# Two channels to a matmul: kernel values, a wider 0/1 spread and a new start in a single-core attention and long-convolution kernel

## The chip, the cores and the metric

One core of one Trainium2 chip. The metric is the time of the kernel on the device in microseconds (us), median over its executions. A program on one core is repeated on the same chip beside the kernel before. Wherever a ratio stands, it is the mean time of one kernel's fast runs over the mean of the other's fast runs of the same rounds, so it is not quite the ratio of the medians quoted beside it; brackets give its 95% interval. A run over 1.5% above the fastest of its kernel counts as slow; the medians and ranges quoted hold slow runs too, the ratios do not. The granted clock is the TensorE clock that a run was given, as a share of full speed.

## The reference

Two independent parts share the core and their outputs are joined:

```python
def _A_ref(x, wqkv, wo):            # x: 1 x 2048 x 640, 32 heads of 20
    W, dil = 8, 2                   # each position sees 8 keys, 2 apart
    ...
    logits = jnp.einsum("bhsd,bhswd->bhsw", q, kg) * scale
    attn = _softmax(masked logits)
    o = jnp.einsum("bhsw,bhswd->bhsd", attn, vg)
    return o... @ wo

def _B_ref(u, A_re, A_im, B_re, B_im, C_re, C_im, log_dt, Dskip):   # u: 1 x 2048 x 640, N = 192 states
    dt = jnp.exp(log_dt)[:, None]
    logdA = dt * (A_re + 1j * A_im)
    dB = dt * (B_re + 1j * B_im)
    P = jnp.exp(logdA[:, :, None] * l[None, None, :])
    K = jnp.einsum("dn,dnl,dn->dl", Cc, P, dB).real      # the "kernel values": 640 x 2048
    y = irfft(rfft(u padded) * rfft(K padded))[:L]       # convolution by FFT
    return y + u * Dskip
```

The change is about K. The kernel writes the exponent l as a coarse plus a fine part, builds an X table (20 coarse entries) and a Y table (33 fine ones) for each channel on VectorE and ScalarE, and gets K as small matrix products X^T Y over the 192 states. 128 of the states fill the partitions, the other 64 of two channels share them.

## The kernel before

The parts that the argument touches. Steps are queued with `st(...)` and put out in the order of a long list, `ORDER` (cut here), that also sets the order on each engine.

```python
    psk = Lazy(lambda: psp.tile([128, 512], f32, name="ps_k"))     # one PSUM bank for all kernel values
    st(lambda: V.memset(psk()[:], 0.0))
    ...
        def go(hf):                                      # a "flip": transposes of 5 chunks on TensorE
            for c in range(NCH):
                ...
                if hf == 0:
                    MM(o, lhsT=nt[:, 0:128], rhs=rhs[:, 0:96], start=True, stop=True, ...)
                    continue
                MM(o[:, 0], lhsT=nt[:, 0:128], rhs=rhs[:, 96:128], start=True, stop=True, ...)
                for h in range(2):                       # two 64-row tiles
                    hs = slice(64 * h, 64 * h + 64)
                    MM(o[hs, 1:3], lhsT=nt[hs, 128:192], rhs=rhs[hs, hs], ..., tile_position=(64 * h, 64 * h))
    ...
    cst = tl("prep", [128, 2, 2, CW], bf16, "cs", tag="cs", bufs=4)   # generators; stored to DRAM
    ...
    def kgen(c):
        t0 = 0
        for nt in (11, 11, 10):
            ps = lambda nt=nt: psk()[:, 0:nt * NB].rearrange("p (t b) -> p t b", b=NB)

            def go(part, t0=t0, nt=nt, ps=ps):
                for i in range(nt):
                    for g in range(4):
                        hb = 64 * (g // 2)
                        rows, col, tp = (slice(0, 128), 32 * g, 0) if part < 2 else (slice(hb, hb + 64), 128 + 32 * (g % 2), hb)
                        MM(ps()[32 * g:32 * g + 20, i, :], lhsT=X[c]()[rows, part % 2, :, col + t0 + i],
                           rhs=Y[c]()[rows, :, part % 2, col + t0 + i], start=(part == 0 and i == 0), stop=(part == 3), tile_position=(tp, 32 * g), ...)

            for part in range(4):
                st(lambda part=part, go=go: go(part))
            st(lambda t0=t0, nt=nt, ps=ps: ACTE.copy(out=Kd[c]()[:, :, t0:t0 + nt], in_=ps().rearrange("p t b -> p b t")))
            t0 += nt
    ...
        for tq in range(4):                              # 0/1 spread: the K values put in place for the FFT
            ts = slice(8 * tq, 8 * tq + 8)
            ps = bank([128, 8, 8, 8], "ps_s", "b")

            def go(ts=ts, ps=ps):
                for j in range(8):
                    for n_, (w, par) in enumerate(plan[j]):
                        sel = slice(0, 8) if par is None else slice(par, 8, 2)
                        for g in range(4):
                            MM(ps()[32 * g:32 * g + 32, j, sel], lhsT=SEL()[:, w, :], rhs=K2()[:, g, sel, ts], ..., tile_position=(0, 32 * g))
    ...
        rc = tl("att", [128, 128], f32, "rc", tag="rc")          # reciprocals of the softmax
        hl = tl("att", [128, 2, 128], bf16, "rhl", tag="rhl")
```

Mind the last index of X and Y in `kgen`: a matmul takes one column (one state-channel slot) out of each of 20 and 33 rows of 192 elements. All its weight columns and all its moving columns are far apart in memory.

The softmax here doesn't subtract the row's maximum and nothing guards it: scores larger than these inputs give would overflow.

## Time and profile before

| | before |
|---|---|
| median of 4 (range) | 380.8 us (376.8 to 384.4) |
| span of the profiled run, granted clock | 376.6 us, 0.879 |
| busy TensorE / VectorE / ScalarE | 300.9 / 312.0 / 274.1 us |
| TensorE idle for instructions ("issue") before ps_k and ps_s | 9.2 and 8.8 us |

VectorE and TensorE are near equally loaded, and neither is full throughout. One stretch that the prediction reads but does not show, as busy time by stretches (from:to us and length; then TensorE, its weight loads, VectorE, ScalarE, GpSimd, each with its count; then granted clock, DMA share, GB/s):

```profile
23.00:60.00 37.00, 18.20 (x49) 6.23 (x49) 36.75 (x87) 34.20 (x88) 5.41 (x8) 0.69 0.69 194
```

VectorE is full (36.75 of 37) while TensorE is half idle.

### The profile page before, as it was taken

To read this page: it belongs to the slowest core of one execution; us is meant where nothing else is said; L and a number is where in the kernel's file an instruction comes from. 1 tells how busy PE (TensorE), PEld (TensorE's weight loads), DVE (VectorE), ACT (ScalarE), POOL (GpSimd) and SP (SyncE) were. 2 spreads that over 40 slices of the span, in tenths; PEclk is the share of its full clock that TensorE was granted. 3 is DMA by queue.
4 is the path that set the end of the run, shared out by engine and by line. 5 is a ranking of instruction groups with operands and counts; after the bars stand their busy time and mean duration, and the time that the engine had idled before them with its cause. 6 is when DMAs were issued, how large, how long until landed. Compare 5 with 4: busy or idle time off the path is not lost. (4 is left out here: it accounts for less than half of the span.)

```text
span 376.6 us, 14749 instructions
## 1 busy us (share of the span) xinstructions
PE 300.9 (80%) x6407; PEld 199.4 (53%) x6420; DVE 312.0 (83%) x468; ACT 274.1 (73%) x602; POOL 62.8 (17%) x123
## 2 busy tenths in 40 slices
PE   3982619989999794857596998889779997999791
PEld 2640204564346441645464786758557685657660
DVE  3379999979999899967866999994582998999970
ACT  2589997999996672456846877869575998977541
POOL 1101121100000000715032200120130102300641
PEclk9987588999999898558967897589899999999996
DMA  7996487763857556497725253325662998997947
GB/s 189 228 272 133 137 265 259 242 213 127 262 176 244 195 164 201 107 257 207 167 76 175 66 196 119 106 58 174 193 170 81 334 316 246 308 300 217 254 104 165
DMA packets 59696, 72.54 MB, mean 193 GB/s; under 512 B 24344, under 2 KB 49544, under 8 KB 58864
## 3 DMA queue, kind: packets, MB, share of 16 engines
q1 hardware_dynamic: 53760, 54.91, 49.0%
q0 software_dynamic: 5296, 15.96, 15.6%
q8 instruction: 50, 0.82, 0.9%
q10 hardware_dynamic: 576, 0.74, 0.6%
q14 instruction: 14, 0.11, 0.1%
HBM read 43.98 MB, written 24.98 MB: 183 GB/s over the span
## 5 line engine op out<-in xcount | busy, mean ns | idle before, releaser
L575 PE MATMUL ps_p<-xT,w 128*128 128x512 bf16 x287 | 75.6, 411 | 22.2 <-ACT st L578 19.7
L575 PEld LDWEIGHTS <-w 128*128 128x128 bf16 x300 | 30.0, 104 | 63.5 <-issue 34.3
L549 PE MATMUL ps_k<-Ytab,Xtab 128*20 128x33 bf16 (+1 forms) x2560 | 53.9, 246 | 11.4 <-issue 9.2
L736 DVE TENSOR_TENSOR prod<-qb,kb 128x2048 bf16<-128x2048 bf16 x40 | 47.7, 1222 | 16.9 <-PE ps_l L741 16.9
L549 PEld LDWEIGHTS <-Xtab 128*20 128x20 bf16 (+1 forms) x2560 | 45.4, 127 | 22.3 <-issue 18.5
L792 DVE TENSOR_TENSOR p<-vb,attn 128x2048 bf16<-128x2048 bf16 x40 | 47.6, 1221 | 11.3 <-PE ps_o L797 11.3
L634 ACT CAST A<-ps_f 128x512 bf16<-128x512 f32 x80 | 43.6, 611 | 18.0 <-PE ps_f L629 16.5
L688 ACT CAST S<-ps_f 128x512 bf16<-128x512 f32 x80 | 43.2, 618 | 10.1 <-PE ps_f L684 7.5
L578 ACT CAST st<-ps_p 128x512 bf16<-128x512 f32 x60 | 33.5, 583 | 6.3 <-PE ps_p L575 6.0
L785 POOL DMA_DIRECT2D vb<-vd x40 | 22.0, 555 | 80.3 <-DVE p L792 78.1
L691 DVE TENSOR_TENSOR Yf<-S 128x1024 bf16<-128x1024 bf16 x40 | 26.1, 686 | 6.5 <-PE ps_ia L705 5.0
L684 PE MATMUL ps_f<-A,cT 128*64 128x128 bf16 x640 | 27.7, 225 | 2.5 <-issue 1.6
L811 PE MATMUL ps_op<-wo,oT 128*128 128x320 bf16 x160 | 26.4, 308 | 0.0
L684 PEld LDWEIGHTS <-cT 128*64 128x64 bf16 x640 | 20.3, 111 | 11.2 <-issue 8.9
L510 ACT ACTIVATE Stab<-ta 128x192 bf16<-128x192 f32 x80 | 25.1, 366 | 0.6 <-DVE Ytab L532 0.6
L711 ACT CAST Z<-ps_ia 128x512 bf16<-128x512 f32 x40 | 22.0, 625 | 2.2 <-PE ps_ia L705 2.0
L741 PE MATMUL ps_l<-prod,cGs 128*32 128x512 bf16 x160 | 18.0, 445 | 7.0 <-DVE prod L736 5.9
L629 PE MATMUL ps_f<-cBD,U 128*64 128x128 bf16 x320 | 22.5, 302 | 0.0
L629 PEld LDWEIGHTS <-U 128*64 128x64 bf16 x320 | 19.6, 205 | 3.6 <-issue 2.8
L705 PE MATMUL ps_ia<-cEA,Yf 64*128 64x128 bf16 x640 | 21.2, 216 | 0.4 <-ACT Z L711 0.2
L188 DVE TENSOR_TENSOR krtmp<-Xtab,Xg 128x1536 bf16<-128x1536 bf16 (+2 forms) x30 | 20.6, 688 | 0.2
L188 DVE TENSOR_TENSOR Xtab<-Xtab,Xg 128x1536 bf16<-128x1536 bf16 (+2 forms) x30 | 20.5, 686 | 0.0
(105 smaller groups left out, 524.2 us busy)
## 6 DMA issues: line engine op xcount, KB each, us to landing
vb<-vd SPq DMA_DIRECT2D x40, 128.5 KB
vb<-vd POOLq DMA_DIRECT2D x40, 128.5 KB, 4.1
Gdram<-cs SPq DMA_DIRECT2D x22, 192.0 KB
HB<-k_HB SPq DMA_DIRECT2D x8, 512.0 KB
Zdram<-Z SPq DMA_DIRECT2D x3, 1024.0 KB
zq<-Zdram SPq DMA_DIRECT2D x12, 256.0 KB
kb<-kd SPq DMA_DIRECT2D x4, 657.5 KB
us<-in_B_u_dram POOLq DMA_DIRECT2D x2, 1280.0 KB, 7.4
```

Of the source, the lines that this page charges most:

```text
L188: step(lambda i=i: V.tensor_tensor(out=(O, t)[i]()[0], in0=Y(), in1=g(i), op=A.mult))
L549: MM(ps()[32 * g:32 * g + 20, i, :], lhsT=X[c]()[rows, part % 2, :, col + t0 + i], rhs=Y[c]()[rows, :, part % 2, col + t0 + i], start=(par ...
L575: MM(ps()[:], lhsT=w()[:, kt, 128 * ct:128 * ct + 128], rhs=xT()[:, kt, 512 * sc:512 * sc + 512], start=(kt == 0), stop=(kt == 4))
L578: st(lambda so=so, sc=sc, ps=ps: ACTE.copy(out=so()[:, sc], in_=ps()[:]))
L629: MM(ps()[64 * r:64 * r + 64, jj], lhsT=src(16 * dd + 4 * jq + jj), rhs=BD1()[:, r, :], start=(jj == 0), stop=True, skip_group_check=True, ...
L634: st(lambda o=o, ps=ps: ACTE.copy(out=A1[c]()[:, :, sig, o:o + 16].rearrange("p k (j g) -> p k j g", g=4), in_=ps()[:].rearrange("p j (k g ...
L684: MM(ps()[64 * dd:64 * dd + 64, kk, r], lhsT=T()[:, k, r, :], rhs=A1[c]()[:, k, :, 64 * dd:64 * dd + 64], start=(kk == 0 and r == 0), stop ...
L688: st(lambda h=h, ps=ps, Sp=Sp: ACTE.copy(out=Sp()[:, :, :, :, 2 * h:2 * h + 2, :].rearrange("p r s j k g -> p (r s) j k g"), in_=ps()[:].r ...
L691: st(lambda b=b, i=i, Sp=Sp: V.tensor_tensor(out=Yf[c]()[:, 2 * i:2 * i + 2, :, 32 * b:32 * b + 32], in0=Sp()[:, :, 1].rearrange("p r j k ...
L736: st(lambda pr=pr, ct=ct, u2=u2: V.tensor_tensor(out=pr()[:], in0=q()[:, ct].unsqueeze(1).to_broadcast([128, 4, PB]), in1=windows(k()[:, c ...
L792: st(lambda p2=p2, u2=u2: V.tensor_tensor(out=p2()[:], in0=v()[:, :, 2 * u2:2 * u2 + PB], in1=attn[b]()[:, u2].unsqueeze(1).to_broadcast([ ...
L811: MM(ps()[:], lhsT=oT[b]()[:, t, 128 * x:128 * x + 128], rhs=wo_sb()[:, t, 320 * eh:320 * eh + 320], start=(t == 0), stop=(t == 4))
```

## The change

Intent: fewer and wider TensorE instructions for K (two channels to a matmul, 40 by 66 columns, two column groups in place of four; a spread with 256 columns), so that TensorE neither issues nor fetches so many (12842 become 9224, by the prediction); a quicker start (matmuls clear the bank, flips grouped by tile shape); and an order made for the new durations. The larger Kd tile takes memory; in return one of four `cs` buffers goes, and the reciprocals share the output tiles' buffers.

```diff
-    st(lambda: V.memset(psk()[:], 0.0))
+    st(lambda: PQ.memset(zf()[:, 0:512], 0.0))
+    def clear():
+        for k in range(11):
+            MM(psk()[:], lhsT=zf()[:, 0:128], rhs=zf()[:, 0:512], start=True, stop=True)
 ...
-                    continue
-                MM(o[:, 0], lhsT=nt[:, 0:128], rhs=rhs[:, 96:128], ...)
+                else:
+                    MM(o[:, 0], lhsT=nt[:, 0:128], rhs=rhs[:, 96:128], ...)
+            for c in range(NCH if hf else 0):        # the 64-row tiles in a loop of their own
 ...
-    Kd = [tl("cst", [128, NB, 32], bf16, "Kd", tag="Kd") ...]
+    Kd = [tl("cst", [128, 2, 2, NB, 16], bf16, "Kd", tag="Kd") ...]
 ...
-            cst = tl("prep", [128, 2, 2, CW], bf16, "cs", tag="cs", bufs=4)
+            cst = tl("prep", [128, 2, 2, CW], bf16, "cs", tag="cs", bufs=3)
 ...
+        def pairs(ap, col):      # 40 weight columns, 96 elements apart: two channels
+            return bass.AP(ap.tensor, ap.offset + col, [list(ap.ap[0]), [96, 40]])
+        def two(ap, col):        # 33 x 2 moving columns, the pair 96 elements apart
+            return bass.AP(ap.tensor, ap.offset + col, [list(ap.ap[0]), list(ap.ap[1]), [96, 2]])
+        for gl in range(2):
+            for nt in (6, 5, 5):
+                        for q in range(2):
+                            rows, col, tp = (slice(0, 128), 32 * q + 16 * gl, 0) if part < 2 else (slice(64 * q, 64 * q + 64), 64 + 16 * gl, 64 * q)
+                            MM(ps()[64 * q:64 * q + 40, i], lhsT=pairs(X[c]()[rows, part % 2], col + t0 + i),
+                               rhs=two(Y[c]()[rows, :, part % 2], col + t0 + i), ..., tile_position=(tp, 64 * q))
 ...
-        for tq in range(4):
-            ps = bank([128, 8, 8, 8], "ps_s", "b")
+        for jp in range(4):
+            ps = bank([128, 2, 8, 2, 16], "ps_s", "b")
 ...
-        rc = tl("att", [128, 128], f32, "rc", tag="rc")
+        rc = tl("att", [128, 128], f32, "rc", tag="ob", bufs=2)
 ...  (hl the same; layouts of Gt, K2 and the DRAM copy of K to suit; ORDER wholly new)
```

The four products of a pair of channels include two mixed ones, which are not wanted and are simply not read.

## The prediction

A "change of mode" in it is a change of the tile shape from one matmul to the next, as between the 128-row and the 64-row ones of its timeline of the flips.

> **What bounds the kernel now.** I read the page's slices, then busy time by stretches, the chain of waits, the waits by engine, the timeline of TensorE, and the groups of instructions.
>
> By stretches (PE, PEld, DVE, ACT, POOL busy us, granted clock, DMA share, GB/s):
>
> ```profile
> 0.00:23.00 23.00, 16.38 (x122) 11.05 (x124) 8.94 (x20) 10.40 (x26) 3.39 (x11) 0.99 0.94 237
> ...
> 60.00:111.00 51.00, 47.40 (x675) 24.91 (x680) 47.83 (x88) 49.88 (x104) 3.89 (x6) 1.00 0.63 206
> 111.00:165.00 54.00, 44.03 (x1028) 27.58 (x1030) 52.15 (x78) 30.31 (x72) 7.64 (x20) 0.82 0.63 190
> 165.00:213.00 48.00, 35.37 (x948) 24.65 (x946) 34.85 (x42) 30.92 (x64) 14.99 (x28) 0.78 0.60 159
> ```
>
> Until 23 us VectorE has 8.9 us of work: it waits for the transposes ("flips") on TensorE. From 23 to 165 us VectorE is full (36.8 of 37, 47.8 of 51, 52.2 of 54). From 165 us no engine is full by its busy time: 35.4 and 34.9 of 48. The chain of waits says what holds it: from 213 us on it is nearly all TensorE, with holes that nothing in the program explains (start, length, what):
>
> ```profile
> 227.12 0.89 PE ps_k L549 x41
> 228.01 0.59 PE ps_f L629 x8
> 228.78 1.67 issue
> 230.45 0.94 PE ps_k L549 x33
> ...
> 240.74 1.83 PE ps_s L665 x73
> 242.57 1.21 PE ps_f L629 x10
> 243.78 2.25 issue
> ```
>
> The waits by engine put 8.8 us before ps_s L665 and 9.2 us before ps_k L549 down to "issue". In the trace's queue records each hole follows a packet of the instruction queue (50 packets, 0.82 MB, so 16 KB each): packets start at 228.05, 243.62, 265.88, 280.25 and 311.32 us, and TensorE goes on 1.3 to 1.6 us after each has landed. The holes are 256 TensorE instructions or a multiple apart. From 111 us on I count fourteen that I read so, some 26 us together, of which 25 come after 165 us or just before. So the second half is bound by TensorE, and a seventh of its time there is spent waiting for its own instructions. The holes come where instructions are short: 256 of them are 128 pairs of weight load and matmul, which ps_k uses up in 2.2 us and ps_s in 1.3, against about 4 us from one block to the next.
>
> [...] in the groups
>
> ```profile
> L684 PEld LDWEIGHTS <-cT 128*64 128x64 bf16 x640 | 20.3, 111 | 11.2 <-issue 8.9
> L629 PEld LDWEIGHTS <-U 128*64 128x64 bf16 x320 | 19.6, 205 | 3.6 <-issue 2.8
> L684 PE MATMUL ps_f<-A,cT 128*64 128x128 bf16 x640 | 27.7, 225 | 2.5 <-issue 1.6
> L549 PE MATMUL ps_k<-Ytab,Xtab 128*20 128x33 bf16 (+1 forms) x2560 | 53.9, 246 | 11.4 <-issue 9.2
> L665 PE MATMUL ps_s<-K,cSEL 128*32 128x64 bf16 (+1 forms) x720 | 9.9, 208 | 8.8 <-issue 8.8
> ```
>
> (the last numbers: busy us, mean ns of one, idle before) 64 weight columns take 111 ns when they are neighbours (T) and 205 when they are 64 bytes apart (U); and a ps_k matmul of 33 columns[...], takes longer (246) than one of 128 neighbours (225).[...]
>
> ```profile
> 8.83 0.24 PE L375 MATMUL ps_tr<-dg,nat 128*128 128x32 bf16 x1
> 9.00 0.32 PE L378 MATMUL ps_tr<-dg,nat 64*64 64x64 bf16 x2
> 9.24 0.24 PE L375 MATMUL ps_tr<-dg,nat 128*128 128x32 bf16 x1
> ```
>
> One chunk's three small matmuls take 0.41 us, with two changes of mode among them.
>
> **The change, part by part.**
>
> *Kernel values (ps_k).* 2560 matmuls of 20 by 33 columns in four column groups become 1280 of 40 by 66 in two. In the timeline, 40 full-height ones take 0.80 us (235.27 to the next group at 236.07) and 80 half-height ones 1.40 (238.17 to 239.57): 20 and 17.5 ns each with the change of mode, 16 to 17 within a burst, so 2560 x 18 = 46 us. A round of four thus takes 66 ns, and it is no slower at half the granted clock (means within a burst 16.8 and 17.0 ns). 33 columns in 66 ns are 2.0 ns a column, near U's weights (two loads a round, 62 ns a matmul, 64 columns in 124 ns: 1.9). I read this as a rate per stream of scattered columns: a matmul is bound by its 33 scattered reads. The new matmul reads 66 columns, scattered too (pairs 192 bytes apart), and only two run side by side: 66 x 1.66 (the rate of the shortest loads: 184 ns for U, 107 to 111 for ps_k, less the common 78) + 12 of turnaround = 122 ns a round, 61 a matmul, 1280 x 61 = 78 us. So halving the instructions makes this stage's matmuls **32 us longer**, not shorter. Half of them (1316 of 2560 by windows) lie in the TensorE-bound stretch: +16 us on the path. The others lie between 60 and 165 us, where TensorE has 14 us idle in 105: +15 fits barely, with VectorE still the bound.
>
> *Instruction blocks.* 12842 TensorE instructions become 9224, 50 blocks become 36, and the densest ones slow down: 128 pairs of the new ps_k take 7.8 us, longer than a block's 4 us. Holes in ps_k and ps_s should go; those amid other short matmuls (31 ns a pair, 4.0 us a block) stay at 0.3 us or so. 25 us become about 5: **-20 us** on the path.
>
> *0/1 spread (ps_s).* 720 matmuls at 8 to 12 ns, some 7 us, become 180 of 256 columns[...]. **-2 us**, its holes being counted above.
>
> *Flips.* 30 chunks of 0.41 us (0.31[...]) lie between 7.9 and 22.2 us. Grouped by shape, each half flip has one change of mode, not nine or ten[...] (the first flip waits until 6.4 us anyway). I estimate 1.0 us a half flip for 2.1 to 1.6, so 5 to 6 us for six; the flip that the phases need comes first. VectorE is full right after, so **-5 us** for all that follows.
>
> *ScalarE.* ps_k is emptied 30 times for 15. From 363 columns in 459 ns and 512 in 611, a column costs 1 ns: 10 x 490 + 20 x 425 = 13.4 us for 6.9. +6.5 us on an engine with 274 of 377: beside other work.
>
> *Transfers.* K2's pieces shrink from 512 to 256 bytes and Kd's store becomes four; hidden, DMA being at 0.6 there. The reciprocals share the output tiles' buffers: a wait of up to 3 us for an output to land, four times, partly on VectorE's path near the end. *New order*: unknown; it is made for the new durations, so I give it 2 us.
>
> Sum on the path: +16 - 20 - 2 - 5 - 2 + 2 (shared buffers) = -11 at best, less what VectorE and the wait for one ps_k bank keep back, which I put at 4: 376.6 becomes 369 or 370. Scaled by the median of 380.8 to that span of 376.6: 373 to 374. I go to 372 for the first rival.
>
> **The rivals.** (1) *The stage is bound by weight columns or by a fixed cost of a round, not by scattered moving columns.* Weight columns: 4 x 20 = 80 in 66 ns before, 2 x 40 = 80 after, so 42 us both times. For it: 0.83 ns a column is also near U's 0.97 if two loads share one path. Against: the shortest ps_k load is 107 ns where four shared ones would give 144. Then the +16 is nil, and VectorE (312 us and its start) is the bound: 354 to 362. (2) *TensorE becomes the bound in the first half too.* With +32 us it needs 301 + 32 - 8 = 325 of busy time plus early idle (some 18), holes (5) and an end where it has 11 idle: 360 at the least; if the ps_k bank is waited for 30 times, if the rate is 2.0 and not 1.66 (+8 us), or if the clock stays low, 380 to 390. For it: VectorE and TensorE are near equal already. (3) *The holes stay*, because a block takes its 4 us whatever the rate and other short matmuls fill in: then +16 - 8 - 7 gives 378. Against: holes stand at 1.3 to 1.6 us after landing, so slower use of a block must shorten them.
>
> **Range and chances.** The terms are large and of opposite sign (+16, -20), each known to some 6 us, so 80% is 356 to 386. 2% below is 373.2, so my estimate lies on that line; rival 1 falls wholly below it, at a quarter. Faster 0.55, same 0.34, slower 0.11.
>
> **What would show it.** Right: ps_k matmuls of some 280 to 300 ns for 246, spaced by about 60; "issue" before ps_s and ps_k below 4 us together; flips over by 16 us; ScalarE's ps_k group at 13 us for 30; VectorE's busy time unchanged at 312. Wrong: ps_k spaced by 33 ns (rival 1), holes of 2 us (rival 3), VectorE no longer full between 60 and 165 us (rival 2).

## More of the kernel before

The kernel before took 377 to 382 us in the different batches, so batches are compared by their ratios.

VectorE hardly waits up to 165 us, as the waits of VectorE between 23 and 165 us say (who waits, for whom: us in total, times, longest):

```profile
DVE cs L454 <- ACT cs L453: 2.6, 2, 2.3
DVE prod L736 <- PE ps_l L741: 1.7, 2, 1.0
DVE pr L414 <- PE ps_tr L378: 0.8, 1, 0.8
```

## The result, and the profile after

| | before | after |
|---|---|---|
| median (range), 4 runs each | 380.8 us (376.8 to 384.4) | 395.3 us (394.6 to 397.7) |
| ratio | | 1.0428 [1.0333, 1.0522] |
| span, granted clock of the profiled run | 376.6, 0.879 | 393.0, 0.901 |
| busy TensorE / VectorE / ScalarE | 300.9 / 312.0 / 274.1 | 336.8 / 313.1 / 280.5 |

The changed kernel is slower, by 4%, outside the predicted range. All its runs are fast ones and its granted clock is higher than before, so the clock is not the reason.

The instructions first. By the trace's records of the ps_k line (name and count: least/median/longest ns, first and last start), before and then after:

```profile
L549 PEld LDWEIGHTS <-Xtab x2560: 107/124/176, 68.6 to 290.6; 64*20 64x20 bf16 x99, 128*20 128x20 bf16 x98
L549 PE MATMUL ps_k<-Ytab,Xtab x2560: 222/244/270, 68.6 to 290.7; 64*20 64x33 bf16 x99, 128*20 128x33 bf16 x98
```

```profile
L572 PEld LDWEIGHTS <-Xtab x1280: 141/149/184, 68.7 to 301.3; 64*40 64x40 bf16 x93, 128*40 128x40 bf16 x90
L572 PE MATMUL ps_k<-Ytab,Xtab x1280: 276/291/351, 68.7 to 301.4; 64*40 64x66 bf16 x93, 128*40 128x66 bf16 x90
```

A matmul takes 291 ns for 244. What counts is how closely they follow each other within a burst, since several run side by side: the starts in the trace are 63.8 ns apart for full-height ones and 59.0 ns for half-height ones, where it was 17.1 and 15.9. (Counting the first and last matmuls of a burst in another way moves these spacings, and those below, by up to 3 ns.) So half as many cost almost four times as much each. One half-height burst of each, and the group after it, in the timeline of TensorE (start, length, count), before and then after: 80 matmuls hold TensorE for 1.40 us, then 12 for 0.84 us.

```profile
238.17 1.47 PE L549 MATMUL ps_k<-Ytab,Xtab 64*20 64x33 bf16 x80
239.57 0.72 PE L629 MATMUL ps_f<-cBD,U 128*64 128x128 bf16 x8
```

```profile
230.86 0.90 PE L572 MATMUL ps_k<-Ytab,Xtab 64*40 64x66 bf16 x12
231.70 0.40 PE L768 MATMUL ps_l<-prod,cGs 128*32 128x512 bf16 x4
```

The groups of instructions say the same (busy us, mean ns | idle just before and for whom); the eviction of the bank (ScalarE's copy of ps_k into Kd), before and then with its matmul after:

```profile
L554 ACT CAST Kd<-ps_k 128x363 bf16<-128x363 f32 (+1 forms) x15 | 6.9, 459 | 9.7 <-PE ps_k L549 9.6
```

```profile
L572 PE MATMUL ps_k<-Ytab,Xtab 64*40 64x66 bf16 (+1 forms) x1280 | 95.5, 300 | 2.4 <-DVE Ytab L547 1.5
...
L577 ACT CAST Kd<-ps_k 128x330 bf16<-128x330 f32 (+1 forms) x30 | 16.1, 536 | 32.7 <-PE ps_k L572 28.3
```

"issue" no longer stands among what the ps_k matmuls wait for: the holes of the instruction fetch are gone there (9.2 us in the kernel before), as meant. ScalarE's evictions have grown from 6.9 to 16.1 us, and its waits for them from 9.6 to 28.3 us. The flips are done by 14.6 us (22.3 before), in two or three blocks of equal shape (timeline of TensorE, start, length, count):

```profile
9.09 0.35 PE L386 MATMUL ps_tr<-cident,nat 128*128 128x32 bf16 x5
9.36 0.47 PE L393 MATMUL ps_tr<-cident,nat 64*64 64x64 bf16 x10
9.76 0.32 PE L386 MATMUL ps_tr<-dg,nat 128*128 128x32 bf16 x5
```

And the stretches, to be held against those of the kernel before:

```profile
0.00:23.00 23.00, 12.59 (x136) 7.63 (x137) 15.32 (x38) 16.07 (x47) 4.69 (x13) 0.90 0.94 217
23.00:60.00 37.00, 23.36 (x84) 8.98 (x83) 31.02 (x68) 29.47 (x71) 4.28 (x6) 0.82 0.75 231
60.00:111.00 51.00, 51.00 (x401) 28.25 (x400) 38.12 (x68) 45.87 (x96) 3.88 (x6) 0.97 0.54 181
111.00:165.00 54.00, 45.84 (x501) 27.78 (x500) 47.72 (x75) 35.21 (x76) 9.43 (x24) 0.88 0.61 188
165.00:213.00 48.00, 46.75 (x808) 36.92 (x808) 40.21 (x53) 36.07 (x81) 7.29 (x13) 0.86 0.47 126
```

VectorE has done 15.3 us of work by 23 us (8.9 before): the new start gives it a lead of 6.4 us. It is lost by 60 us (46.3 us done for 45.7), and then turned round: 84.5 for 93.5 by 111 us, 132.2 for 145.7 by 165 us. In the stretch from 60 to 111 us TensorE is busy for 51.0 of 51 us. VectorE's waits between 23 and 165 us, after:

```profile
DVE ph L465 <- ACT cs L467: 9.1, 6, 2.8
DVE prod L763 <- PE ps_l L768: 5.6, 3, 2.7
DVE cs L469 <- ACT am L451: 3.9, 2, 2.6
DVE cs L469 <- ACT cs L468: 2.4, 4, 1.1
```

So VectorE now waits mostly for ScalarE. A tempting story follows: ScalarE stands at its evictions until TensorE has filled the bank (28.3 us of waits in all), and VectorE then waits for ScalarE. The experiments show that this is the symptom and not the cause.

### The profile page after: what moved, and what is told of

The parts are those of the page before. It is cut to its first block, busy times and chain, and to the rows that moved or that the text cites.

```text
span 393.0 us, 11172 instructions
## 1 busy us (share of the span) xinstructions
PE 336.8 (86%) x4611; PEld 225.2 (57%) x4611; DVE 313.1 (80%) x467; ACT 280.5 (71%) x617; POOL 63.6 (16%) x123
## 3 DMA queue, kind: packets, MB, share of 16 engines
q1 hardware_dynamic: 55128, 54.40, 46.5%
## 4 chain that ended last, share of the span: by engine, by line
PE 53%; ACT 16%; DMA 14%; DVE 7%; SPq 6%; issue 3%; ACTq 0%; DVEq 0%
PE ps_k L572 22%; PE ps_p L605 13%; PE ps_op L838 4%; DMA xT<-in_A_x_dram 4%; PE ps_f L659 3%; SPq L333 3%; ACT S L715 3%; DMA uq<-Udram 3%; PE ps_f L711 3%; ACT A L664 3%; DVE p L819 2%; PE ps_ia L732 2%; PE ps_l L768 2%; DMA vb<-vd 2%; PE ps_ib L901 2%
## 5 line engine op out<-in xcount | busy, mean ns | idle before, releaser
L572 PE MATMUL ps_k<-Ytab,Xtab 64*40 64x66 bf16 (+1 forms) x1280 | 95.5, 300 | 2.4 <-DVE Ytab L547 1.5
L572 PEld LDWEIGHTS <-Xtab 64*40 64x40 bf16 (+1 forms) x1280 | 73.7, 152 | 23.3 <-issue 19.5
L819 DVE TENSOR_TENSOR p<-vb,attn 128x2048 bf16<-128x2048 bf16 x40 | 47.7, 1220 | 11.6 <-PE ps_o L824 8.6
L664 ACT CAST A<-ps_f 128x512 bf16<-128x512 f32 x80 | 42.0, 628 | 5.5 <-PE ps_f L659 5.2
L577 ACT CAST Kd<-ps_k 128x330 bf16<-128x330 f32 (+1 forms) x30 | 16.1, 536 | 32.7 <-PE ps_k L572 28.3
L711 PE MATMUL ps_f<-A,cT 128*64 128x128 bf16 x640 | 31.4, 239 | 1.7 <-ACT S L715 1.1
L711 PEld LDWEIGHTS <-cT 128*64 128x64 bf16 x640 | 23.8, 121 | 10.4 <-issue 9.1
L659 PEld LDWEIGHTS <-U 128*64 128x64 bf16 x320 | 21.1, 202 | 4.9 <-issue 2.5
L732 PE MATMUL ps_ia<-cEA,Yf 64*128 64x128 bf16 x640 | 23.3, 231 | 0.3 <-ACT S L715 0.3
L824 PE MATMUL ps_o<-p,cG 128*32 128x512 bf16 x160 | 17.5, 439 | 6.5 <-DVE p L819 6.5
L732 PEld LDWEIGHTS <-Yf 64*128 64x128 bf16 x640 | 20.4, 102 | 4.3 <-issue 4.0
```

Of the source, the lines that this page charges most:

```text
L572: MM(ps()[64 * q:64 * q + 40, i], lhsT=pairs(X[c]()[rows, part % 2], col + t0 + i), rhs=two(Y[c]()[rows, :, part % 2], col + t0 + i), star ...
L659: MM(ps()[64 * r:64 * r + 64, jj], lhsT=src(16 * dd + 4 * jq + jj), rhs=BD1()[:, r, :], start=(jj == 0), stop=True, skip_group_check=True, ...
L664: st(lambda o=o, ps=ps: ACTE.copy(out=A1[c]()[:, :, sig, o:o + 16].rearrange("p k (j g) -> p k j g", g=4), in_=ps()[:].rearrange("p j (k g ...
L711: MM(ps()[64 * dd:64 * dd + 64, kk, r], lhsT=T()[:, k, r, :], rhs=A1[c]()[:, k, :, 64 * dd:64 * dd + 64], start=(kk == 0 and r == 0), stop ...
L732: MM(ps[dd]()[:, jj].rearrange("p l r -> p (l r)"), lhsT=Yf[c]()[d, q, 4 * jq + jj, :], rhs=EA()[d, q, :], start=(jj == 0 and q == 0), sto ...
L819: st(lambda p2=p2, u2=u2: V.tensor_tensor(out=p2()[:], in0=v()[:, :, 2 * u2:2 * u2 + PB], in1=attn[b]()[:, u2].unsqueeze(1).to_broadcast([ ...
```

## The experiments

Three things were to be told apart: what the ps_k matmuls cost and why (a1 to a4), how the cost reaches the end (c3, e1), and what the other parts gave or took (the rest).

### Back to one channel, neighbouring columns: a1, a2, a3, a4

a1 is the changed kernel, in its own order, with one channel to a matmul again:

```diff
-  MM(ps()[64 * q:64 * q + 40, i], lhsT=pairs(X..., col + t0 + i), rhs=two(Y..., col + t0 + i), tile_position=(tp, 64 * q))
+  for s_ in range(2):
+      o_, w_ = 64 * q + 32 * s_, col + 96 * s_ + t0 + i
+      MM(ps()[o_:o_ + 20, i], lhsT=X[c]()[rows, part % 2, :, w_], rhs=Y[c]()[rows, :, part % 2, w_], tile_position=(tp, o_))
```

> The changed kernel, its order kept, with one channel to a kernel-value matmul again (2560 of 20 by 33 in four column groups, 30 evictions of half the size). Theory A (33 scattered moving columns set the pace, and pairing doubles them): matmuls spaced by 16 to 17 ns again, ps_k about 43 us of TensorE for 78, time down by 15 to 25 us from 395, to 370 to 380; holes of the instruction blocks come back in part. Theory B (the new order is what costs): time stays within 5 us of 395.

Measured: 373.3 us (371.1 to 373.9), ratio 0.9822 [0.9751, 0.9893]. That is 6.1% of the kernel before, some 23 us, less than the changed kernel. The spacing is 19.3 and 15.2 ns again, and 4.9 us of "issue" come back before ps_k. So pairing is what makes the changed kernel slower than the kernel before. (This is net of 5.8 us of "issue" that TensorE still waits in a1 and no longer in the changed kernel.) Since a1 and the changed kernel have the same VectorE work in the same order, the work VectorE has done by some time says how far each is. Two stretches of a1:

```profile
60.00:111.00 51.00, 47.31 (x655) 24.31 (x664) 40.77 (x73) 48.03 (x103) 3.88 (x6) 0.94 0.62 204
111.00:165.00 54.00, 45.20 (x943) 28.77 (x947) 53.90 (x82) 37.96 (x84) 13.33 (x30) 0.87 0.68 199
```

With 13.18 and 33.15 us of VectorE before them, a1 has done 87.1 us by 111 us and 141.0 by 165, the changed kernel 84.5 and 132.2. So by 165 us pairing has cost 8.8 us, and of the 24.1 us between the two spans (393.0 and 368.9) the other 15 are lost later. The 6 us by which a1 itself is behind the kernel before at 111 us (93.5) are not the pairs' doing. By 165 us a2, a3 and a4, which follow, have done 141.8, 135.8 and 141.7 us: the dearer the ps_k matmuls of a pair of channels, the less VectorE has done.

a2 keeps the pairs and takes 66 neighbouring moving columns; a3 takes 40 neighbouring weight columns. Both compute wrong values on purpose (the comparison passed a3 all the same: it is loose on this part, so a3's pass says nothing).

```diff
 a2:  def two(...):   [list(ap.ap[0]), list(ap.ap[1]), [96, 2]]  ->  [list(ap.ap[0]), [2, 33], [1, 2]]
 a3:  def pairs(...): [list(ap.ap[0]), [96, 40]]                 ->  [list(ap.ap[0]), [1, 40]]
```

> The changed kernel with the 66 moving columns of each kernel-value matmul taken from neighbouring places (numbers wrong on purpose); weights still scattered. Theory A: the pace is then set by the 40 scattered weight columns, 40 x 1.66 + 12 = 78 ns a round of two, some 40 ns a matmul for 61, and matmuls of about 195 ns for 291. Rival (weight columns or a fixed cost of the round set the pace): stays at 60.

> The changed kernel with the 40 weight columns of each kernel-value matmul taken from neighbouring places (numbers wrong on purpose); moving columns still scattered. Theory A: stays at 58 to 64 ns a matmul. Rival (weight columns set the pace): falls below 40.

Measured, one run each (state unknown): a2 361.1 us, a3 381.6 us. Trace records of the line, a2 and then a3:

```profile
L572 PEld LDWEIGHTS <-Xtab x1280: 140/162/182, 70.0 to 270.5; 64*40 64x40 bf16 x93, 128*40 128x40 bf16 x90
L572 PE MATMUL ps_k<-Ytab,Xtab x1280: 191/235/266, 70.0 to 270.5; 64*40 64x66 bf16 x93, 128*40 128x66 bf16 x90
```

```profile
L572 PEld LDWEIGHTS <-Xtab x1280: 92/114/158, 68.0 to 291.2; 64*40 64x40 bf16 x93, 128*40 128x40 bf16 x90
L572 PE MATMUL ps_k<-Ytab,Xtab x1280: 267/287/304, 68.0 to 291.3; 64*40 64x66 bf16 x93, 128*40 128x66 bf16 x90
```

Neighbouring moving columns bring the spacing from about 61 to 36.0 ns, neighbouring weights only to 54. The weight load itself falls from 149 to 114 ns, but it was not what held the matmul. So the moving operand's scattered columns are the limit, as the prediction read from the kernel before, and its rival 1 (weight columns alone) is out. The weights are not nothing, though: the forecast for a3 was 58 ns or more, and its single run is 14 us under the changed kernel.

a4 does it with right numbers: ScalarE writes the generators and the falling exponentials with the two channels of a pair side by side, so that the Y table holds the pairs as neighbours. VectorE's work on them stays elementwise.

```diff
 def two(ap, col):
-    return bass.AP(ap.tensor, ap.offset + col, [list(ap.ap[0]), list(ap.ap[1]), [96, 2]])
+    return bass.AP(ap.tensor, ap.offset + 2 * col, [list(ap.ap[0]), list(ap.ap[1]), [1, 2]])
 # ScalarE's outputs for generators 8 to 128 (cs, am) and for Stab, e.g.
-    ACTE.activation(out=Stab[c]()[:, k - 1], in_=ta()[:, CW * c:CW * c + CW], ...)
+    ACTE.activation(out=Stab[c]()[:, k - 1].rearrange("p (m h) -> p h m", h=2), in_=ta()[...].rearrange("p (h m) -> p h m", h=2), ...)
```

> The changed kernel with the two channels of a pair put side by side in the Y table (generators of 8 to 128 and the falling exponentials written interleaved by ScalarE; numbers right)[...]. Theory A[...] the 40 scattered weights (78 ns a round) set the pace: some 40 ns a matmul for 61, 27 us less TensorE work, time 370 to 380. If each column that is not next to several others costs: stays at 60 ns and 395 us.

Measured: 365.1 us (363.3 to 367.2), ratio 0.9603 [0.9531, 0.9675]: 8% faster than the changed kernel and 4% faster than the one before.

```profile
L583 PE MATMUL ps_k<-Ytab,Xtab x1280: 216/243/282, 69.8 to 273.7; 64*40 64x66 bf16 x93, 128*40 128x66 bf16 x90
```

A half-height burst of 12, with the group after it:

```profile
216.68 0.61 PE L583 MATMUL ps_k<-Ytab,Xtab 64*40 64x66 bf16 x12
217.23 0.40 PE L779 MATMUL ps_l<-prod,cGs 128*32 128x512 bf16 x4
```

The spacing is 36.0 ns, as in a2, though every pair is still 384 elements from the next. So two neighbours gain here as much as sixty-six. What holds both at 36 ns is not shown, since no run has neighbours in both operands; it may be the 40 scattered weights. In the FFT of the kernel before (ps_f L629, neighbouring moving columns) matmuls follow each other after some 56 ns with the 64 scattered weight columns of U, and with the neighbouring ones of K after 27.9 in bursts at a granted clock of 1.00 and 46 to 51 in most at 0.5; at U's rate 40 columns would take 35 ns (an estimate from these spacings). With one column from each place the spacing was 61 ns; whether 36 ns is the least that it can be, no run shows.

### Is it ScalarE's wait at the bank? c3 and e1

If VectorE is late because ScalarE stands at evictions, then evictions that wait for nothing must give the time back. In both runs the 30 evictions keep their size and place, though not their time, and read something else. Their outputs are wrong, which doesn't matter for the times.

```diff
-  ACTE.copy(out=Kd[c]()[:, :, gl, :, t0:t0 + nt], in_=ps().rearrange("p t b s -> p s b t"))
+  c3: in_=Y[c]()[:, :, 0, 0:2 * nt].rearrange("p b (s t) -> p s b t", s=2)
+  e1: in_=ta()[:, 0:nt * NB * 2].rearrange("p (t b s) -> p s b t", b=NB, s=2)
```

> The changed kernel, where the 30 evictions of ps_k read the Y table in place of the bank: as many, as large, in the same place, but ScalarE no longer waits for TensorE there, nor TensorE for ScalarE. The numbers are wrong on purpose. Theory (the loss reaches VectorE through ScalarE's waits in order): ScalarE's 28 us of waits there go, VectorE's waits for ScalarE between 23 and 165 us fall from about 20 us to under 8, and the time falls by 10 us or more, to 375 to 385. Rival (TensorE's own capacity between 60 and 165 us is what binds, and the waits of ScalarE and VectorE only show it): 390 to 396 us, with VectorE's busy time by 165 us still near 132 us.

Measured: 400.4 us (399.8 to 406.7), ratio 1.0608. It gains nothing, but the run is not clean: reading the Y table held its buffer, and VectorE waited 10.9 us, once, for the next load into it. e1 reads a table that never changes:

> The changed kernel, where the 30 evictions of ps_k read a constant table (ta, f32, as many columns) in place of the bank: ScalarE and TensorE don't wait for each other there, and no buffer of a table is held. Numbers wrong on purpose. Theory (TensorE's own time is the bound in the first half): 388 to 396 us, TensorE's busy time by 165 us within 5 us of the changed kernel's 132.8 and VectorE's within 6 us of its 132.2. Rival (the loss goes through ScalarE's waits): 370 to 384 us with VectorE's busy time by 165 us near 145.

Measured: 392.8 us (391.5 to 394.9), ratio 1.0346 [1.0279, 1.0414] against the changed kernel's 1.0428 [1.0333, 1.0522]; the intervals overlap. The stretches of e1:

```profile
23.00:60.00 37.00, 22.89 (x84) 8.86 (x83) 33.36 (x74) 30.38 (x75) 4.28 (x6) 0.88 0.77 226
60.00:111.00 51.00, 49.66 (x399) 27.95 (x399) 37.98 (x68) 47.95 (x99) 3.88 (x6) 1.00 0.57 192
111.00:165.00 54.00, 46.96 (x508) 28.30 (x507) 47.80 (x76) 38.02 (x77) 9.20 (x23) 0.85 0.60 187
```

With its first line (13.02 us of VectorE and 13.19 of TensorE by 23 us) VectorE has done 132.2 us by 165 us and TensorE 132.7: to half a us the changed kernel's 132.2 and 132.8. And ScalarE's waits between 23 and 165 us, in the changed kernel and then in e1:

```profile
ACT Kd L577 <- PE ps_k L572: 12.0, 10, 3.5
ACT st L608 <- PE ps_p L605: 7.2, 9, 4.3
```

```profile
ACT st L608 <- PE ps_p L605: 11.8, 9, 3.6
ACT attn L771 <- PE ps_l L768: 6.1, 1, 6.1
```

The wait at ps_k is gone and has become a wait at other things that TensorE makes (the projections ps_p, the logits ps_l). TensorE is just as far as before, so everybody who needs it is just as late. This run isn't clean either: its evictions took 25.8 us in place of 16.1, of which 10.1 and 6.4 fall before 165 us. But the waits taken away there are 12.0 us against 3.7 us of added work, and nothing came of the difference. With a2 and a4, where the same 30 evictions stayed and cheaper matmuls gave the first half back, the reading is that the loss is TensorE's own time in the first half, and that the wait of ScalarE at the bank (28.3 us) is only where it showed.

### The start: b1, c1, c2, d5

b1 is the kernel before, in its own order, with the two parts of the new start; c1 has the grouped flips alone, c2 the clearing matmuls alone (the diffs are those of the change).

> The kernel before, its order kept, with only the first part of the change: the bank cleared by 11 matmuls and the half flips grouped by tile shape. Theory: flips end by 16 us for 22, VectorE has 4 to 6 us more done by 23 us, time 372 to 377 for 380.8. Rival (the start is bound by ScalarE or the inputs' landing, so nothing is gained): 379 to 382.

Measured: 363.2 us (358.0 to 368.1), ratio 0.9508 [0.9405, 0.961]. In its batch that is 14 us by the medians, and 18.6 by the two fast runs alone, where 4 to 9 were expected of it (the kernel before took 377.0 there). VectorE is 8.0 us earlier from the first generator on, which is not 14. Step by step, in b1's profile (a slow run), 6 us of this are left between 60 and 165 us; by 211 us it is 14. So the rest is won between 165 and 211 us, where the kernel before has its largest holes.

> The kernel before, in its own order, with the flips grouped by tile shape and nothing else. Together with the clearing matmuls this gave 363.2 us (-14), with every VectorE step from the first generator on 8.0 us earlier. Theory: the lead comes from the grouping alone (fewer changes of tile shape), so this run stands at 361 to 367 us with the same 8 us lead. Rival: the clearing matmuls do it[...]; then this run stays at 372 to 378 us with a lead of under 3 us.

> The kernel before, in its own order, with the bank cleared by 11 matmuls in place of VectorE's memset and nothing else. Theory (grouping does it): 375 to 381 us, VectorE's steps within 2 us of the kernel before. Rival (the clearing matmuls do it): 361 to 367 us, steps 5 to 8 us earlier.

Measured: c1 376.2 us, ratio 0.9973 [0.9884, 1.0061]; c2 370.6 us, ratio 0.9802 [0.9721, 0.9883]. Theory and rival both miss. c1 does have the lead: 15.8 us of VectorE's work by 23 us for 8.9. But by 60 us 4 us of it are gone: VectorE then waits 3.3 us for the transfer of u, and the DMA share there is 0.96. c2 has hardly a lead (9.95 us by 23 us), yet it gains. (With the clears the first ten flips take 1.00 us, for 1.78 before and in c1. But over the first 23 us c2's granted clock is 0.75, for 0.99 before and 1.00 in c1.) The wait for "issue" before the 0/1 spread, 8.8 us in the kernel before, in c1 and then in c2:

```profile
PE ps_s L669 <- issue: 9.7, 4, 4.6
```

```profile
PE ps_s L670 <- issue: 2.1, 3, 1.2
```

In the trace of the kernel before the holes stand 256 TensorE instructions or a multiple apart (up to 3.7 us each), and 11 clears with their weight loads put 22 more at the front. d5 puts the same 22 there without any work to speak of, and keeps the memset:

```diff
+  for k in range(11):
+      MM(psk()[:, 0:1], lhsT=zf()[:, 0:128], rhs=zf()[:, 0:1], start=True, stop=True)
   # after V.memset(psk()[:], 0.0)
```

> The kernel before with its memset, and 11 matmuls of a single column of zeros at the start: the same 22 instructions more on TensorE as the clearing matmuls, but hardly any work[...]. Theory (the 22 instructions move the ends of the instruction blocks out of the 0/1 spread): 368 to 374 us, holes at ps_s between 165 and 213 us under 1 us together, as with the clears. Rival[...]: 376 to 382 us with holes at ps_s as before, 6.6 us in that stretch.

Measured: 373.5 us (371.4 to 379.3), ratio 0.9837 [0.9752, 0.9921]. So the shift alone gives about what the clears give (1.6 and 2.0%, with intervals that overlap). Its profile fell in a slow run, which is why only the place of the holes is read from it, not their sum: between 160 and 220 us

```profile
PE ps_f L689 <- issue: 5.2, 2, 4.0
PE ps_k L554 <- issue: 3.1, 2, 2.4
PE ps_s L670 <- issue: 1.7, 1, 1.7
```

The holes before ps_s have shrunk (6.6 us in the kernel before from 165 to 213) and others have come before ps_f. My figure of under 1 us was too low. The gain does fall where a hole was: VectorE's steps are within 0.7 us of the kernel before until 159 us and 4.5 us earlier at 171, and the kernel before has a hole of 3.7 us at 165. It looks like luck, not design: 22 instructions put the holes elsewhere, and what another number of them would do was not run. Why c1 and c2 give 0.3 and 2.0% and both together 4.9% is settled only in part: c1 lost its lead to the transfer of u, for which b1 did not wait. b1 also has the widest scatter of all runs, and its ratio rests on two fast runs.

### The wide spread: b2

b2 is b1 with the 0/1 spread of the change (256 columns, a quarter of the matmuls; five steps of the order moved to suit).

> The same with the 0/1 spread in matmuls of 256 columns too (180 for 720; five of its steps moved so that no value is read before it is written). Theory: the holes of the instruction blocks before ps_s go (8.8 us in the kernel before), others stay before ps_k; 5 to 9 us less than with the start alone: 364 to 371. Rival (these holes are hidden behind other engines): within 2 us of the start alone.

Measured: 355.9 us (352.8 to 358.0), ratio 0.9411 [0.9332, 0.9491]. It is the best kernel, 6% faster than the one before and 10% faster than the changed one. "issue" before ps_s has gone from its waits. Against b1's fast runs (359.3 us) it gains 3.6 us, between my theory and the rival, and the intervals overlap. TensorE's busy time is 289.9 us for 295.9 in b1's slow run. The stretch that had the largest holes, where the kernel before had 35.37 and 34.85 us of TensorE and VectorE:

```profile
165.00:213.00 48.00, 42.98 (x1138) 31.93 (x1136) 44.20 (x63) 39.68 (x85) 13.37 (x26) 0.93 0.65 179
```

### The order and the buffers: a5, a6, a7, d2, d3, d4, e2

a5 puts the changed program into the order of the kernel before, step for step; because the reciprocals share buffers there, seven output steps had to move. a6 is the same with a4's neighbouring pairs, a7 with one channel to a matmul.

> The changed kernel's program in the order of the kernel before (each old kernel-value step carries the new ones that cover it; seven steps of output tiles moved so that shared buffers do not lock). Theory A (pairing scattered columns is the cost, not the order): 388 to 402, near 395. Theory B (the new order is the cost): 375 to 384.

> The changed kernel with interleaved pairs (365 us in its own order) in the order of the kernel before. If the new order is worth something: 368 to 376. If it is worth nothing: 362 to 367.

> The changed program with one channel to a matmul again (it took 373.3 us in the changed kernel's order), put in the order of the kernel before. It differs from the best experiment so far (355.9 us: the kernel before with the new start and the wide spread) only by the 30 small evictions for 15, the layout of the stores and of K2, and the shared buffers of the reciprocals. Theory: the new order is made for the slow matmuls and costs the quick ones about 15 us; then this run takes 355 to 362 us. Rival: what costs is the 30 evictions, the layout and the shared buffers, whatever the order; then 370 to 378 us.

Measured: 425.5, 395.4 and 397.9 us; ratios 1.1226, 1.0484 and 1.0552. All three are 7 to 9% of the kernel before slower than in the new order, and all my figures were too low. Their granted clocks are low too (0.82 to 0.88, for 0.89 to 0.92 in the new order); whether that is a cause or only goes with the waits is not shown. My theory for a7, that the new order is made for slow matmuls, is wrong: a7 has the quick ones and still loses. So part of the program other than the pairs must suit the old order badly. a7's waits name a candidate: ScalarE waits 11.2 us for stores of `cs` to land. That is the buffer the change took away. d3 takes it from b2 alone; d2 and d4 give it back to a7 and a1 (there is room with one channel, since half of Kd is unused).

```diff
 d3:      cst = tl("prep", ..., "cs", tag="cs", bufs=4)  ->  bufs=3
 d2, d4:  bufs=3 -> 4, and Kd [128, 2, 2, NB, 16] -> [128, 1, 2, NB, 16]
```

> The best kernel so far (355.9 us) with three cs buffers in place of four, as the changed kernel has, and nothing else. Theory: with three, a generator waits for the store of the one three before it to land (ScalarE's waits for that were 11 us between 23 and 165 us in the changed program under the old order, with 15 us of VectorE's waits after it), so this run takes 380 to 398 us. Rival (the small evictions, the layout or the shared buffers cost it): 355 to 362 us.

> The changed program with one channel to a matmul, in the order of the kernel before (397.9 us), with four cs buffers again; there is room, since with one channel half of the Kd tile is unused. Theory (the third buffer was the loss): 356 to 364 us. Rival (30 evictions, layout, shared buffers): 385 to 398 us.

> The changed kernel with one channel to a matmul, in its own order (373.3 us), with four cs buffers. If the new order is made to live with three buffers, the fourth gives under 4 us: 369 to 374 us. If three buffers cost the changed kernel too, it comes near the old order with four: 357 to 364 us.

Measured: d3 368.8 us, ratio 0.9732 [0.9669, 0.9794] for b2's 0.9411; d2 383.5 us, 1.0104 [1.0017, 1.0191] for a7's 1.0552; d4 367.9 us, 0.9715 [0.9642, 0.9788] for a1's 0.9822 [0.9751, 0.9893]. Having only three buffers costs 3.2% (12 us) in the old order by d3 and 4.5% by d2; d3's own figure was 380 or more, so it is less than I thought. d2's theory (356 to 364 us) fails. In the new order it costs some 1%, and the intervals of a1 and d4 overlap: the new order seems to have made room for it. How it costs, in d3 (ScalarE's and VectorE's waits between 23 and 165 us; b2 has no wait of the first kind and 3.4 us of the second):

```profile
ACT cs L461 <- DMA Gdram<-cs: 12.6, 4, 6.7
```

```profile
DVE cs L463 <- ACT cs L462: 10.2, 6, 4.1
```

d2 still has 27 us on b2. e2 is d2 with buffers of their own for the reciprocals, and so without the seven moved steps:

> The changed program with one channel to a matmul, four cs buffers, in the order of the kernel before (383.5 us), and with buffers of their own for the reciprocals, so that the seven steps that had been moved for the sharing are back in their places. If sharing is what costs: 358 to 368 us. If the 30 small evictions, the half-width stores and the K2 layout cost it: 377 to 384 us.

Measured: 367.9 us (367.3 to 370.9), ratio 0.9718 [0.9656, 0.978]. Sharing, with the moves it forces, costs 3.9% (15 us) in the old order. Nearly all of it falls after 165 us (VectorE idle for 45.2 us there in d2, for 30.1 in e2). A part shows near the end in d2 as VectorE's wait for an output to land, which e2 does not have:

```profile
DVE rc L794 <- DMA out_dram<-ob: 6.8, 2, 3.6
```

What stays between e2 and b2 (0.9718 and 0.9411, 3% or 12 us) is the rest of the change by one channel: 30 evictions for 15, the narrower pieces of K's way through DRAM, and the layout of Gt and K2. It was not split further. With buffers enough, the old order is as good as the new one: e2 stands at 0.9718, d4, in the new order and with shared buffers, at 0.9715. In the changed kernel's own profile the shared buffers cost VectorE's reciprocals nothing (its only wait before them is 0.2 us, for TensorE), and the wait of `cs` is 3.4 us: the new order hides the first and most of the second.

### All runs

| run | what it is | median us | ratio to before |
|---|---|---|---|
| after | the changed kernel | 395.3 | 1.0428 |
| a1 | after, one channel | 373.3 | 0.9822 |
| a2 / a3 | after, neighbouring moving columns / weights (wrong values) | 361.1 / 381.6 | single runs |
| a4 | after, pairs side by side | 365.1 | 0.9603 |
| a5 / a6 / a7 | after / a4 / a1 in the old order | 425.5 / 395.4 / 397.9 | 1.1226 / 1.0484 / 1.0552 |
| c3 / e1 | after, evictions that wait for nothing (wrong values) | 400.4 / 392.8 | 1.0608 / 1.0346 |
| b1 | before, new start | 363.2 | 0.9508 |
| c1 / c2 / d5 | before, grouped flips / clears / 22 idle instructions | 376.2 / 370.6 / 373.5 | 0.9973 / 0.9802 / 0.9837 |
| b2 | b1 and the wide spread | 355.9 | 0.9411 |
| d3 | b2, three cs buffers | 368.8 | 0.9732 |
| d4 | a1, four cs buffers | 367.9 | 0.9715 |
| d2 / e2 | a7, four cs buffers / and own buffers for the reciprocals | 383.5 / 367.9 | 1.0104 / 0.9718 |

## Why the prediction was wrong, point by point

It said 372 and it was 395. Against a1 the miss of 23 us splits in two: pairing cost 23 to 24 us and not the 16 on the path, and everything else gave 7 us (a1 against the kernel before) and not 23 (-20 - 2 - 5 - 2 + 2 + 4). Where in time it lies, VectorE's idle time says, since busy and idle time together are the span (us, from the stretches of the profiled runs):

| | before | b2 | a1 | after |
|---|---|---|---|---|
| VectorE idle until 165 us | 19.3 | 13.6 | 24.0 | 32.8 |
| VectorE idle after 165 us | 45.3 | 28.7 | 28.9 | 47.1 |
| VectorE busy | 312.0 | 311.6 | 316.0 | 313.1 |

After 165 us the prediction was nearly right: it had +16 for the pairs and -22 for the rest (-18 if all that is kept back falls there), and it came to +18.2 (after against a1) and -16.4 (a1 against before). Until 165 us it was wrong: it had VectorE full and 5 us ahead, and VectorE stood idle for 13.5 us more. Of these, 8.8 are the pairs'. The other 4.7 stand in a1 too, in place of the 5 to be won.

- **The cost of a paired matmul: right.** 61 ns were predicted, 59.0 and 63.8 were measured, and a2 and a4 (36.0 ns in both) show that it is the scattered moving columns. Rival 1 is out.
- **"+15 fits barely, with VectorE still the bound": failed.** The prediction set 15 us of new TensorE work between 60 and 165 us against 14 us of idle time there and let it cost nothing. It cost 8.8 us (VectorE's work by 165 us, a1 against the changed kernel). TensorE had been busy for 47.4 of the 51 us from 60 to 111 us, so the room was not where the work came; the work made it full there (51.0 of 51), and what it should have handed on came late to VectorE in the next stretch (47.7 of 54 us busy for 53.9 in a1). This is rival 2, beyond its own 380 to 390; it had been named and given too little weight.
- **"+16 on the path" in the second half: right**, 15 us of the span (18.2 of idle time, less 2.9 of VectorE's busy time). In e1, without ScalarE's waits at the bank, the idle time after 165 us is 46.6 us for 47.1, so they had no visible part in it.
- **Holes -20: right in kind, and about right in worth after 165 us.** TensorE's waits for "issue" are 25.2 us in the kernel before, 5.8 in a1 and none in the changed kernel, and a1 has 16.4 us less idle time of VectorE after 165 us, though no run gives the holes' share of that alone. What the prediction did not see is that the place of the holes can move with the count of instructions ahead of them: 22 instructions at the start are worth 1.6% by themselves (d5), so a part of the holes is to be had without any change of the matmuls. Rival 3 (the holes stay) is out.
- **Flips -5, "VectorE is full right after": failed in the changed kernel.** The lead is 6.4 us by 23 us. In the order of the kernel before, with the clears, it lasts: by 165 us VectorE has done 151.2 us in b1 and 151.4 in b2, for 145.7. With the grouping alone (c1) half of it goes in the wait for the transfer of u. In the new order it is gone by 60 us, in a1, d4 and the changed kernel alike (46.3 to 46.5 us done, for 45.7), while e2 (d4's program in the old order, with own buffers for the reciprocals) has done 50.4. So there it is the new order that gives it away: in the changed kernel VectorE waits 5.2 us for ScalarE between 23 and 60 us.
- **Spread -2:** an estimate of mine; it measured 1.0% of the kernel before between b1 and b2 by their ratios (3.6 us by the fast runs), with intervals that overlap; it holds the holes at ps_s, which the prediction counted apart.
- **ScalarE +6.5 "beside other work": mis-sized, with no harm shown.** 16.1 us of evictions, not 13.4 (536 ns each and not 447), with 28.3 us of waits; taking the waits away gave nothing that can be told from zero (e1, whose evictions were slower).
- **Shared buffers +2 and order -2: both far off.** In the old order the shared buffers cost 3.9% and the loss of the fourth cs buffer, which the prediction passed over though the diff has it, 3.2%; with one channel the new order is worth 7% (a7 against a1) and wins about that back; the old order with buffers enough (e2) does as well as the new one (d4). The 30 evictions and the layouts, in the sum only as ScalarE's time, cost 3% there (e2 against b2).

So the parts beside the pairs could give 6% (b2), but with what was added to serve the pairs (a Kd twice as large, hence a buffer less and sharing, twice the evictions, and the new order) 2% of it are left in a1, and the pairs then turn that into a loss. How the 4% between a1 and b2 splits in the new order is open: there only the fourth buffer was tried, at 1% with overlapping intervals (d4).

## What to carry to other kernels

Merging two scattered operands into one matmul halved the instructions here (2560 to 1280) but not the reads: with the columns scattered and two column groups in place of four, the wider matmuls followed each other after 59.0 to 63.8 ns for 15.9 to 17.1. With the pair laid side by side in memory it was 36.0 ns, which was worth 8% (a4). Before new work is booked as hidden in an engine's idle time, look at the fullest stretch it falls in, not at the sum over a long one; and when an engine shows the new waits, test whether it is the cause by letting it wait for nothing. Count what a change must give up to fit (buffers, sharing), and try its cheap parts alone: here two of them without the main one made the best kernel.
